# Zero matmuls from the start, two masks by ACT and Pool, and w_in's first columns slot by slot in a retention and gated-MLP kernel

## The chip, the cores and the metric

The kernel runs on one core of a Trainium2 chip. The metric is device time in microseconds (us) for the whole launch: 214.74 us is the median of 13 runs before the change, which lie between 213.97 and 215.69 us. The engines are named as the profile names them: PE is TensorE's matmul row and PEld its weight loads, DVE is VectorE, ACT is ScalarE, POOL is GpSimd, and SP is SyncE, which here only issues DMAs.

## The reference, cut to what matters

```python
def _attn_ref(q, k, v):                    # q, k, v: (4, 8, 768, 64)
    gamma = 1.0 - 2.0 ** (-5.0 - np.arange(H))
    scale = 1.0 / np.sqrt(D)
    for t in range(S):
        state = gamma * state + k[:, :, t] (outer) v[:, :, t]
        y[:, :, t] = scale * (q[:, :, t] @ state)

x = y.transpose(0, 2, 1, 3).reshape(3072, 512)
h = x @ w_in                               # (512, 2048)
g = h * np.cos(h)
out = g @ w_out                            # (2048, 512)
```

## The kernel before

The 768 steps of the recurrence are cut into 6 chunks of 128. A **slot** p is one chunk of two of the four batches (b = 0, 1), with all 8 heads: there are 12 slots, and slots 0 and 1 are the first chunks of the two pairs of batches. Two slots make a **group** g of 512 tokens, which is what one matmul of the MLP takes as its moving side. There are 6 groups.

In a slot, q and k are transposed on PE (`t_mm`) and copied out of PSUM by DVE or ACT (`t_copy`, the tile qkt), `a_mm` multiplies k and q to the scores of even and odd heads (j = 0, 1), these are masked, `y_mm` multiplies masked scores and v (and, after the first chunk, adds the state's share), `s_mm` updates the state, and ACT copies y into the tile xt (`y_copy`). In slots 0 and 1 the mask is the table of decays `dec`, v is only cast (`raw_v`, "rv"), and the scaled v (`conv_v`) is made later on Pool for the state. All matmul inputs are bf16.

The MLP of a group takes 16 blocks of 128 columns of w_in. For a block, `f_mm` is four matmuls of 512 tokens (line 401); `h_mm` takes two blocks for one slot's 256 tokens with eight matmuls of 256 (line 422). ACT then makes the cosine (`f_cos`), DVE the product (`f_mul`, `h_mul`, into the tile gt), and `o_mm` multiplies with w_out (line 446).

The work of slots 0 to 5 and of groups 0 and 1 is put in order by `Plan`, a list scheduler that runs while the program is built. Each operation has engines, a cost, predecessors, tokens (7 PSUM banks, 3 cosine buffers, 8 DMA semaphores, one port shared by DVE and POOL) and a rank; the lowest rank that is ready is taken. A unit of `h` or `f` has rank 1000 and more and yields to work of rank below 20 that comes ready within 0.6. What comes out is a fixed order for each engine; on the chip only semaphores hold an instruction back. `COLD` is the time up to which the planner doubles PE's costs. The fourth argument of `run` is the **fill**: between the two times PE gets matmuls on a tile of zeros (`idle_mm`, line 472) wherever nothing is ready, each counted as 0.12. They too stand in the fixed order, and write to a bank that is then overwritten.

The planner knows of loads by assumed landing times: the first four in the list `map(at, ...)` on line 522, the others in the order of `LOADS` from the second argument of `Plan` on. POOL issues the loads of slots 0 to 7 and of the weights: K of slot 0, then Q1, K1, v0, v1 (slots 0 and 1), the first quarter of w_in in two halves (w0a, w0b), the second and third quarters (w1, w2), then q2 and so on. `HOLD` keeps q2 behind the products named by `SPLIT`.

`SPLIT` names masks (p, b, j) that DVE doesn't do: ACT copies the bank to SBUF (`a_save`, line 345) and POOL multiplies with `dec` (`a_late`, line 349). Before the change this is (1, 0, 1) alone. `HALF0` is the number of blocks of w_in that slots 0 and 1 take by `h_mm`, each as soon as its own y is copied; the blocks from `HALF0` to 15 go by `f_mm`, which needs both slots' y. Before the change `HALF0` is 0. From group 2 on, the loop at the end of the function interleaves `f_mm`, `o_mm` and the slots by hand.

Of the kernel before, what the change touches and what calls it, by code (L numbers as in the profile page):

```python
# [28 lines left out]
class Plan:  # L29
# [16 lines left out]
    def add(self, engines, cost, fn, after=(), rank=0.0, take=(), give=(), mode=None,  # L46
            spare=0, mb=0.0, rate=0.0, lag=0.0, name=""):
        op = dict(engines=engines, cost=cost, fn=fn, after=[a for a in after if a], rank=rank,
                  take=take, give=give, mode=mode, spare=spare, mb=mb, rate=rate, lag=lag,
                  n=len(self.ops), start=None, done=None, free=None, name=name)  # L50
        self.ops.append(op)
        return op
# [91 lines left out]
            op["fn"](op["eng"])  # L144


HALF0, SPARE, RF, RM, COLD = 0, 1, 40.0, 40.0, 8.5


@with_exitstack  # L150
def kernel(
# [9 lines left out]
    nc = tc.nc  # L161
    B, H, S, D = q.shape
# [24 lines left out]
    def sb(shape, dt, name):  # L187
        return const.tile(shape, dt, name=name)
# [29 lines left out]
    zero = sb([128, 256], BF16, "zero")  # L218
# [13 lines left out]
    def kb(p):  # L232
        return kx if p == 1 else ks[p % NB]
# [6 lines left out]
    def load(eng, p, names):  # L240

        bp, c = divmod(ORDER[p], NC)
        for n in names.split():
            t, src = SRC[n[0].lower()]
            if len(n) == 1:
                t = (qs[p % NB] if n == "Q" else kb(p)) if n in "QK" else t[p % PRE]
                eng.dma_start(  # L247
                    out=t.rearrange("p b h d -> p (b h) d"),
                    in_=src[ds(2 * bp, 2), :, ds(c * C, C), :].rearrange(
                        "b h t d -> t (b h) d"))  # L250
            else:
                b = int(n[1])
                eng.dma_start(
                    out=t[p % PRE][:, b],
                    in_=src[2 * bp + b, :, ds(c * C, C)].rearrange("h t d -> t h d"))
# [22 lines left out]
    def conv_q(p, b, e):  # L278
        if p < 2:
            copy(e, qs[p % NB][:, b], qf[p % PRE][:, b])  # L280
            return
        ENG[e].tensor_tensor(out=qs[p % NB][:, b], in0=qf[p % PRE][:, b],  # L282
                             in1=bc(gq, ORDER[p] % NC), op=ALU.mult)

    def conv_v(p, b, e):
        ENG[e].tensor_tensor(out=vb(p)[:, b], in0=vf[p % PRE][:, b],  # L286
                             in1=bc(gk, ORDER[p] % NC), op=ALU.mult)

    def raw_v(p, b, e):
        copy(e, vr[p][:, b], vf[p % PRE][:, b])  # L290

    def conv_k(p, b, e):
        copy(e, ks[p % NB][:, b], kf[p % PRE][:, b])
# [41 lines left out]
    def a_mask(p, b, j):  # L335
        bank = held["a", p, b][j]
        nc.vector.tensor_tensor(  # L337
            out=am[p % 2][b][j], in0=bank.rearrange("p (a t) -> p a t", a=HP),
            in1=(dec[:, j] if p < 2 else mask.unsqueeze(1).to_broadcast([128, HP, 128])),
            op=ALU.mult)  # L340
        banks.give(bank)

    def a_save(p, b, j):
        bank = held["a", p, b][j]
        nc.scalar.copy(out=amf[b], in_=bank)
        banks.give(bank)

    def a_late(p, b, j):
        nc.gpsimd.tensor_tensor(out=am[p % 2][b][j],
                                in0=amf[b].rearrange("p (a t) -> p a t", a=HP),  # L350
                                in1=dec[:, j], op=ALU.mult)
# [26 lines left out]
    def has_s(p):  # L378
        return p != 1 and (p == LATE or ORDER[p] % NC < NC - 1)
# [87 lines left out]
            (nc.sync, nc.scalar)[hf].dma_start(  # L467
                out=out[ds(o_row(g, j), C), ts(hf, 256)], in_=o[:, ts(hf, 256)])

    def idle_mm(e):  # L470
        bank = banks.take()
        nc.tensor.matmul(bank[:, :256], lhsT=zero[:, :128], rhs=zero, start=True, stop=True)  # L472
        banks.give(bank)


# [5 lines left out]
                   allow_small_or_imprecise_dtypes=True)  # L481
    load(nc.sync, 0, "q0 q1")
    load(nc.gpsimd, 0, "K")
    nc.vector.memset(lnsc, math.log(scale))
    nc.vector.memset(halfpi, math.pi / 2.0)

    nc.vector.tensor_tensor(
        out=dist.rearrange("p (a b) -> p a b", a=8),
# [10 lines left out]
    for j in range(2):  # L499
        for a in range(HP):  # L500
# [2 lines left out]
    nc.scalar.activation(out=gq, in_=lgp, func=AF.Exp, bias=lnsc)  # L503
    nc.scalar.activation(out=gk, in_=lgp, func=AF.Exp, scale=-1.0)
    nc.scalar.activation(out=lnsc, in_=halfpi, func=AF.Sin)
    nc.vector.memset(zero, 0.0)


    PL = 6
    ASEP = 4  # L510
    CD = "P"
    SPLIT = {(1, 0, 1)}
    HOLD = "q2", "o2"
    plan = Plan({"bank": 7, "cos": 3, "sem": 8, "out": 4, "port": 1}, 6.0)
    add = plan.add
    SB2 = {"D": (0.33, 0.42), "A": (0.49, 0.585)}
    TT = {"D": (0.6, 0.69), "P": (1.03, 1.05)}
    PS = {"D": (0.6, 0.69), "A": (0.49, 0.585)}
    ld = {}
    prev = None  # L520
    at = lambda tm: dict(start=0.0, free=0.0, done=tm, lat=0.0)
    ld["q", 0, 0], ld["q", 0, 1], ld["k", 0, 0], ld["k", 0, 1] = map(at, (3.9, 5.0, 6.5, 6.5))
    LOADS = ["Q1", "K1", "v0", "v1", "w0a", "w0b", "w1", "w2", "q2", "k2", "w3a", "v2", "w3b", "q3", "k3", "v3",
             "o0", "o1", "o2", "o3", "q4", "k4", "v4", "q5", "k5", "v5", "q6", "k6", "v6",
             "q7", "k7", "v7"]
    LAG = {"w1": 0.8}
    pend = []
    for i, x in enumerate(LOADS):
        if x[0] in "qkvQK":
            p = int(x[1:])  # L530
# [6 lines left out]
        elif x[0] == "w":  # L537
# [4 lines left out]
                    mb=(524288e-6 if w else 1048576e-6), rate=(390e-3 if w else 415e-3),  # L542
                    lag=LAG.get(x, 0.0), name=x)
            for f in range(lo // 128, lo // 128 + (2 if w else 4)):
# [7 lines left out]
    T = {}  # L552
# [3 lines left out]
    for p in range(PL + 2):  # L556
        c = ORDER[p] % NC

        for b in range(2):
            if p == 1:  # L560
                T["cq", p, b], T["ck", p, b] = ld["q", p, b], ld["k", p, b]
            else:
                T["cq", p, b] = add("D" if p < 2 else "DP" if p < 3 else "P", SB2 if p < 2 else TT,
                                    lambda e, p=p, b=b: conv_q(p, b, e),
                                    [ld["q", p, b], G("tq", p - NB, b), G("dt", p - NB, 0)],
                                    10 * p + b, [("port", 1)], [("port", 1)], name="cq%d%d" % (p, b))
            if p == 0:
                T["ck", p, b] = ld["k", p, b]
            elif p > 1:
                T["ck", p, b] = add("A", SB2, lambda e, p=p, b=b: conv_k(p, b, e),  # L570
                                    [ld["k", p, b], G("tk", p - NB, b), G("dt", p - NB, 1), G("s", p - NB)],
                                    10 * p + b, name="ck%d%d" % (p, b))
            cd = add(CD if p == 2 else "P", TT, lambda e, p=p, b=b: conv_v(p, b, e),
                     [ld["v", p, b], G("y", p - NB, b), G("s", p - NB)],
                     10 * p + 1.5 + b + (20 if p == 0 else 60 if p == 1 else 0),
                     [("port", 1)], [("port", 1)], name="cv%d%d" % (p, b))
            T["cd", p, b] = T["cv", p, b] = cd
            if p < 2:
                T["cv", p, b] = add("AD"[b], SB2, lambda e, p=p, b=b: raw_v(p, b, e), [ld["v", p, b]],
                                    10 * p + 2.5 + b, [("port", 1)] if b else [], [("port", 1)] if b else [],  # L580
                                    name="rv%d%d" % (p, b))
# [31 lines left out]
        for b in range(2):  # L613
            for j in range(2):
                if (p, b, j) in SPLIT:
                    o = add("A", (0.49, 0.585), lambda e, p=p, b=b, j=j: a_save(p, b, j),
                            [T["a", p, b]], 0, (), [("bank", 1)],
                            name="ms%d%d%d" % (p, b, j))
                    T["m", p, b, j] = add("P", (1.03, 1.05), lambda e, p=p, b=b, j=j: a_late(p, b, j),
                                          [o], 0, [("port", 1)], [("port", 1)],  # L620
                                          name="ml%d%d%d" % (p, b, j))
                    continue
                T["m", p, b, j] = add("D", (0.6, 0.69), lambda e, p=p, b=b, j=j: a_mask(p, b, j),
                                      [T["a", p, b], G("y", p - 2, b)], 10 * p + 1 + b,
                                      (), [("bank", 1)], name="m%d%d%d" % (p, b, j))
# [13 lines left out]
        else:  # L639
            T["y", p, 0] = T["y", p, 1] = add(  # L640
                "E", 2 * yt + 0.25 * (has_s(p)),
                lambda e, p=p: (y_mm(p, 0), y_mm(p, 1), s_mm(p) if has_s(p) else None),
# [41 lines left out]
    for b in range(2):  # L684
        T["cd", 0, b]["after"] += [T["cv", 1, 1]]
        T["cd", 1, b]["after"] += [T["cd", 0, 1]]
    hold["after"] += [T[("m",) + x] for x in SPLIT]
    for j in range(4):
        for part in range(4):
# [6 lines left out]
                                  "full", name="o%d.%d" % (j, part))  # L696
        add("A", (0.49, 0.585), lambda e, j=j: o_out(0, j, e), [T["o", j, 3]], 300, (),
            [("bank", 1)], name="oc%d" % j)
    plan.run({"S": 2.5, "P": 3.2, "A": 5.5, "D": 3.6, "E": 1.0}, COLD, 0.6, (5.0, 16.0, 0.12, idle_mm))
    plan.emit()  # L700

    for p in (PL + 2, PL + 3):
# [30 lines left out]
    for g in range(2, NG + 1):  # L733
        for s in range(16):
            hf, r = divmod(s, 8)
            p = 2 * (g + 1) + hf
# [46 lines left out]
```

## Time and profile before

| what | value |
|---|---|
| median of 13 runs | 214.74 us |
| the profiled execution's own time | 214.35 us |
| its span, first to last instruction | 212.6 us |
| PE busy from 16 to 32 us of the span | 16.00 of 16.00 us |
| DVE busy from 12 to 16 us | 3.55 us |
| POOL busy from 12 to 16 us, then from 16 to 36 us | 1.76 us, then 19.92 us |
| first `f_mm`, by the chain of waits | 18.09 us |
| fifth `f_mm` (block 4), by the same chain and the spacing in it | 21.9 us |

The time outside the span, 214.35 - 212.6 = 1.75 us, belongs to the launch and isn't covered by the trace. A busy PE says little here before 18 us, because the matmuls on zeros count as busy. The useful work is found by line: 308 (transposes), 331 (scores), 362 and 367 (y), 387 (state), 401 and 422 (w_in), 446 and 463 (w_out); line 472 is the zeros.

### The profile page before, as it was taken

The numbers are of one execution on the slowest core, as the hardware profiler recorded it, in microseconds if no ns is written. First come the engines' busy times: TensorE is split into PE (matmuls) and PEld (weight loads), VectorE is DVE, ScalarE is ACT, GpSimd is POOL, SyncE is SP. The second block draws the span as 40 slices with busy tenths as digits, with TensorE's granted clock in tenths as the row PEclk, the third lists the DMA queues.
The fourth block names the chain that finished last, engine by engine and source line by source line (L and its number), as shares of the span: only waits on it lengthen the run. The fifth ranks groups of instructions, "written<-read, shape, count | busy, mean of one in ns | idle before, by whom it ended". The sixth has DMA issues, their size and how long they took to land.

```text
span 212.6 us, 4219 instructions
## 1 busy us (share of the span) xinstructions
PE 202.7 (95%) x1694; PEld 111.5 (52%) x1694; DVE 115.8 (54%) x199; ACT 115.9 (55%) x193; POOL 78.7 (37%) x83
## 2 busy tenths in 40 slices
PE   1799999999999999999999999999999999999993
PEld 1585456798565445445445445445445444444462
DVE  6492899977845635735736736637633333333000
ACT  7475787788663247437447547545545444554120
POOL 8939999999997006533333000000000000000000
PEclk9999999999999999999999999999999999999999
DMA  7999999999997289999993412311011101110212
GB/s 121 199 249 236 299 325 209 222 345 341 345 189 214 85 194 246 240 215 278 149 255 113 96 49 68 85 49 54 0 49 49 52 0 49 49 51 3 99 65 83
DMA packets 57492, 32.00 MB, mean 151 GB/s; under 512 B 46592, under 2 KB 51968, under 8 KB 57472
## 3 DMA queue, kind: packets, MB, share of 16 engines
q0 software_dynamic: 14352, 15.47, 33.0%
q1 hardware_dynamic: 42976, 16.13, 30.8%
q8 instruction: 13, 0.21, 0.4%
q10 hardware_dynamic: 144, 0.13, 0.2%
q14 instruction: 7, 0.06, 0.1%
HBM read 27.26 MB, written 6.29 MB: 158 GB/s over the span
## 4 chain that ended last, share of the span: by engine, by line
PE 92%; ACT 2%; DMA 2%; DVE 1%; issue 1%; SPq 0%; DVEq 0%
PE bank L446 38%; PE bank L401 32%; PE bank L422 5%; PE bank L331 3%; PE bank L472 3%; PE bank L308 3%; PE bank L362 3%; PE bank L367 3%; DMA qf<-in_q_dram 2%; PE bank L463 2%; PE st_ps L387 1%; ACT cosb L409 1%; ACT ks L271 1%; DVE qs L273 1%; ACT xt L271 0%
## 5 line engine op out<-in xcount | busy, mean ns | idle before, releaser
L409 ACT ACTIVATE cosb<-bank,halfpi 128x512 bf16<-128x512 f32 x96 | 65.3, 687 | 59.1 <-PE bank L401 55.3
L446 PE MATMUL bank<-w_out_sb,gt 128*128 128x512 bf16 x368 | 90.9, 379 | 0.0
L413 DVE TENSOR_TENSOR gt<-bank,cosb 128x512 bf16<-128x512 f32 x80 | 54.2, 688 | 58.5 <-ACT cosb L409 58.1
L401 PE MATMUL bank<-xt,w_in_sb 128*128 128x512 bf16 x320 | 80.7, 379 | 0.0
L446 PEld LDWEIGHTS <-gt 128*128 128x128 bf16 x368 | 35.6, 98 | 42.4
L401 PEld LDWEIGHTS <-w_in_sb 128*128 128x128 bf16 x320 | 30.5, 98 | 35.2
L286 POOL TENSOR_TENSOR vs<-vf,gk 128x512 bf16<-128x512 f32 x22 | 22.7, 1046 | 10.8 <-DMA vf<-in_v_dram 4.4
L282 POOL TENSOR_TENSOR qs<-qf,gq 128x512 bf16<-128x512 f32 x18 | 18.5, 1044 | 21.7 <-DMA qf<-in_q_dram 21.6
L337 DVE TENSOR_TENSOR am<-bank,mask 128x512 bf16<-128x512 f32 x40 | 24.9, 681 | 1.2 <-PE bank L331 1.0
L271 ACT COPY ob<-bank 128x512 f32<-128x512 f32 (+1 forms) x24 | 13.8, 577 | 17.5 <-PE bank L446 15.9
L273 DVE CAST stb<-st_ps 64x512 bf16<-64x512 f32 x17 | 11.7, 686 | 11.6 <-PE st_ps L387 11.4
L271 ACT CAST xt<-bank 128x512 bf16<-128x512 f32 x24 | 12.9, 589 | 8.7 <-PE bank L367 8.7
L422 PE MATMUL bank<-xt,w_in_sb 128*128 128x256 bf16 x128 | 15.1, 273 | 0.5 <-ACT xt L271 0.5
L422 PEld LDWEIGHTS <-w_in_sb 128*128 128x128 bf16 x128 | 12.2, 98 | 2.0 <-issue 0.6
L271 ACT CAST ks<-kf 128x512 bf16<-128x512 f32 x20 | 11.5, 621 | 0.2 <-DMA kf<-in_k_dram 0.2
L430 DVE TENSOR_TENSOR gt<-bank,cosb 128x512 bf16<-128x512 f32 x16 | 10.4, 683 | 2.2 <-ACT cosb L409 2.2
L308 PE MATMUL bank<-ident,qs 128*128 128x128 bf16 x48 | 5.2, 250 | 5.5 <-DVE qs L273 5.5
L362 PE MATMUL bank<-qkt,stb 128*64 128x128 bf16 x160 | 10.3, 222 | 0.0
L367 PE MATMUL bank<-am,vs 128*64 128x128 bf16 x160 | 10.0, 219 | 0.0
L362 PEld LDWEIGHTS <-stb 128*64 128x64 bf16 x160 | 8.7, 110 | 2.4 <-issue 1.9
L247 POOL DMA_DIRECT2D vf<-in_v_dram x8 | 9.4, 1182 | 0.0
L367 PEld LDWEIGHTS <-vs 128*64 128x64 bf16 x160 | 8.9, 110 | 0.0
(59 smaller groups left out, 116.8 us busy)
## 6 DMA issues: line engine op xcount, KB each, us to landing
out_dram<-ob SPq DMA_DIRECT2D x23, 256.0 KB, 2.0
vf<-in_v_dram POOLq DMA_DIRECT2D x8, 512.0 KB, 8.3
qf<-in_q_dram POOLq DMA_DIRECT2D x6, 512.0 KB, 9.3
kf<-in_k_dram POOLq DMA_DIRECT2D x6, 512.0 KB, 9.2
w_out_sb<-in_moe_w_out_dram POOLq DMA_DIRECT2D x4, 512.0 KB, 10.2
qf<-in_q_dram SPq DMA_DIRECT2D x4, 512.0 KB, 4.7
kf<-in_k_dram SPq DMA_DIRECT2D x4, 512.0 KB, 6.5
vf<-in_v_dram SPq DMA_DIRECT2D x4, 512.0 KB, 6.7
```

Source lines behind the costliest of these rows:

```text
L271: nc.scalar.copy(out=out, in_=in_)
L273: ENG[e].tensor_copy(out=out, in_=in_)
L282: ENG[e].tensor_tensor(out=qs[p % NB][:, b], in0=qf[p % PRE][:, b], in1=bc(gq, ORDER[p] % NC), op=ALU.mult)
L286: ENG[e].tensor_tensor(out=vb(p)[:, b], in0=vf[p % PRE][:, b], in1=bc(gk, ORDER[p] % NC), op=ALU.mult)
L337: nc.vector.tensor_tensor(out=am[p % 2][b][j], in0=bank.rearrange("p (a t) -> p a t", a=HP), in1=(dec[:, j] if p < 2 else mask.unsqueeze(1 ...
L362: nc.tensor.matmul(yp[ts(j, 64), a, :], lhsT=stb[p % 2][:, b, a, ts(j, 64)], rhs=qt(n, b, a), start=True, stop=False, skip_group_check=True)
L367: nc.tensor.matmul(yp[ts(j, 64), a, :], lhsT=v_[:, b, 2 * a + j, :], rhs=am[p % 2][b][j][:, a, :], start=(c == 0), stop=True, skip_group_c ...
L401: nc.tensor.matmul(bank, lhsT=w_in_sb[:, i, ts(f, 128)], rhs=xt[g % 2][:, i, :], start=(i == 0), stop=(i == KIN - 1))
L409: nc.scalar.activation(out=cb, in_=bank, func=AF.Sin, bias=halfpi)
L413: nc.vector.tensor_tensor(out=gt[g % 2][:, f, :], in0=bank, in1=cb, op=ALU.mult)
L422: nc.tensor.matmul(bank[:, ts(e, 256)], lhsT=w_in_sb[:, i, ts(f + e, 128)], rhs=xt[g % 2][:, i, ts(hf, 256)], start=(i == 0 and e == 0), s ...
L446: nc.tensor.matmul(bank, lhsT=gt[g % 2][:, f, ts(j, 128)], rhs=w_out_sb[:, f, :], start=(f == 0), stop=(f == KOUT - 1))
```

## The change

The tile of zeros is set before the other small constants, and seven matmuls on it, each 512 columns wide (the zeros read twice over), are put on PE ahead of the plan. The planner's PE starts at 4.2 instead of 1.0, its doubled cost ends at 5.2 instead of 8.5, and fills are allowed from 4.2 to 18.0 instead of from 5.0 to 16.0. `HALF0` becomes 4: blocks 0 to 3 of w_in are done for slot 0 and slot 1 apart. A second mask, (0, 1, 1), is split between ACT and POOL. The other edits change what the planner assumes: K of slot 0 lands at 7.4 instead of 6.5, the other loads run from 6.5 instead of 6.0, w1 has no additional lag, the POOL product costs 1.1 to 1.2 instead of 1.03 to 1.05; and slot 2's q is converted on DVE only.

```diff
-HALF0, SPARE, RF, RM, COLD = 0, 1, 40.0, 40.0, 8.5
+HALF0, SPARE, RF, RM, COLD = 4, 1, 40.0, 40.0, 5.2
...
-    def idle_mm(e):
+    def idle_mm(e, n=1):
         bank = banks.take()
-        nc.tensor.matmul(bank[:, :256], lhsT=zero[:, :128], rhs=zero, start=True, stop=True)
+        nc.tensor.matmul(bank[:, : 256 * n].rearrange("p (n t) -> p n t", n=n),
+                         lhsT=zero[:, :128], rhs=zero.unsqueeze(1).to_broadcast([128, n, 256]),
+                         start=True, stop=True)
         banks.give(bank)
...
     load(nc.gpsimd, 0, "K")
+    nc.vector.memset(zero, 0.0)
     nc.vector.memset(lnsc, math.log(scale))
...
-    nc.vector.memset(zero, 0.0)
+    for i in range(7):
+        idle_mm("E", 2)
...
-    CD = "P"
-    SPLIT = {(1, 0, 1)}
+    CQ, CD = "D", "P"
+    SPLIT = {(1, 0, 1), (0, 1, 1)}
...
-    plan = Plan({"bank": 7, "cos": 3, "sem": 8, "out": 4, "port": 1}, 6.0)
+    plan = Plan({"bank": 7, "cos": 3, "sem": 8, "out": 4, "port": 1}, 6.5)
...
-    ld["q", 0, 0], ld["q", 0, 1], ld["k", 0, 0], ld["k", 0, 1] = map(at, (3.9, 5.0, 6.5, 6.5))
+    ld["q", 0, 0], ld["q", 0, 1], ld["k", 0, 0], ld["k", 0, 1] = map(at, (3.9, 5.0, 7.4, 7.4))
...
-    LAG = {"w1": 0.8}
+    LAG = {}
...
-                T["cq", p, b] = add("D" if p < 2 else "DP" if p < 3 else "P", SB2 if p < 2 else TT,
+                T["cq", p, b] = add("D" if p < 2 else CQ if p < 3 else "P", SB2 if p < 2 else TT,
...
-                    T["m", p, b, j] = add("P", (1.03, 1.05), lambda e, p=p, b=b, j=j: a_late(p, b, j),
+                    T["m", p, b, j] = add("P", (1.1, 1.2), lambda e, p=p, b=b, j=j: a_late(p, b, j),
...
-    plan.run({"S": 2.5, "P": 3.2, "A": 5.5, "D": 3.6, "E": 1.0}, COLD, 0.6, (5.0, 16.0, 0.12, idle_mm))
+    plan.run({"S": 2.5, "P": 3.2, "A": 5.5, "D": 3.6, "E": 4.2}, COLD, 0.6, (4.2, 18.0, 0.12, idle_mm))
```

## The prediction

> **What bounds the kernel now.** I read the page's totals, then the chain of waits in order of time, then the timelines of the first 20 us, engine by engine. The totals, and PE's busy tenths in 40 slices of 5.3 us:
>
> ```profile
> span 212.6 us, 4219 instructions
> PE 202.7 (95%) x1694; PEld 111.5 (52%) x1694; DVE 115.8 (54%) x199; ACT 115.9 (55%) x193; POOL 78.7 (37%) x83
> ...
> PE   1799999999999999999999999999999999999993
> ```
>
> PE is busy in every slice but the first, second and last, and its timeline shows only 0.45, 0.18 and 0.15 us of idle between 18 us and the end. So the end comes at the moment when useful matmuls start to flow, plus their sum. What can be won lies ahead of that moment. The chain there (start, length, engine, tile, line):
>
> ```profile
> 5.40 1.10 DVE qs L273
> ...
> 6.55 0.61 PE bank L308 x4
> 7.16 0.85 PE bank L472 x4
> 8.02 0.85 PE bank L308 x8
> 8.87 0.64 PE bank L472 x3
> 9.51 0.96 PE bank L331 x12
> 10.47 0.97 PE bank L308 x8
> ...
> 14.73 1.60 PE bank L472 x13
> 16.33 0.57 PE bank L367 x16
> 16.89 1.20 PE bank L472 x10
> 18.09 2.59 PE bank L401 x12
> ```
>
> From 6.55 us on PE never pauses, so a late instruction delays all behind it: a fill, too, is work in a fixed order. 4 + 3 fills stand at 0.213 us each (0.85/4, 0.64/3), eight transposes cost 0.85 or 0.97; later ten fills take 1.20 (0.12 each), and the chain has eight transposes at 12.18 us in 0.45. The switch is seen in one fill's duration (min/median/max ns) in two windows:
>
> ```profile
> L472 PE MATMUL bank<-zero x4: 421/421/421, 7.6 to 9.1; 128*128 128x256 bf16 x4
> ...
> L472 PE MATMUL bank<-zero x6: 272/273/401, 11.2 to 11.9; 128*128 128x256 bf16 x6
> ```
>
> PE thus runs at half speed up to some 11.4 us, 4.9 us after its unbroken work began. The last useful gap is the 1.20 us of fills before the first `f_mm`: they wait for ACT, which copies slot 1's y in 1.07 us.
>
> ```profile
> 14.24 1.28 POOL L349 TENSOR_TENSOR am<-gt 128x512 bf16<-128x512 f32 x1 [3.85 <-ACT gt L345]
> ...
> 14.55 1.07 ACT L271 CAST xt<-bank 128x512 bf16<-128x512 f32 x2 [0.39 <-PE bank L367]
> ...
> 16.71 1.07 ACT L271 CAST xt<-bank 128x512 bf16<-128x512 f32 x2 [0.57 <-PE bank L367]
> ```
>
> Slot 0's y is in xt at 15.6 us, and the zeros run while nothing may use it. The loads allow an earlier start: issue plus time to landing gives 7.2 us for K of slot 0, 8.9 for Q1, 10.5 for K1, 12.05 for v0, 13.6 for v1, 14.85 for w0a, 16.2 for w0b, 19.5 for w1, 21.85 for w2.
>
> **The change, part by part.**
>
> *Zeros first.* The memset costs 0.165 us on DVE and goes into DVE's wait for Pool's iota (idle 0.30 us before 1.20), so nothing moves. Seven matmuls of 512 columns cost twice a half-speed fill, 0.43 us, 3.0 together: from about 1.1 to 4.1 us. The first transposes wait for the cast of q until 4.31 anyway. Cover gone, each tenth of overrun is a tenth on the first transposes, which have 1.2 us to spare before the second q arrives. When does full speed come? By the row, 4.9 us after 1.1: at 6.0 us, provided the hole ahead of 6.55 us (some 0.9 us in which PE has run out of planned fills) does no harm. The Trainium skill, "TensorE: Matmul & The Clock Gate", Part 1, speaks against counting on a time: the gate watches a free-running window of about 3.4 us, so opening comes one to two windows after steady work starts, at 4.5 to 7.9 us, and if the hole spoils a window, one later. This trace can't show the phase; its 4.9 us lies inside one to two windows. With the row, everything from 6.55 us on is at full speed. With 7.9, the fills from 6.77 to 7.9 run half as fast: about 5 instead of 9, so 4 x 0.12 = 0.5 us later; with the spoiled window (some 9.9 us) the 14 fills and the eight transposes pay 14 x 0.09 + 0.4 = 1.7 us, which eats the gain. I take the row.
>
> *PE's order up to block 4, by count from the code and duration from the chain.* The second q's transposes stay at 6.55 us (cast of 1.09 us after a landing at 5.38), 0.22 long at full speed (the row at 26.34). The planner believes them done near 5.7 and K at 7.4: (7.4 - 5.7)/0.12 = 14 fills, 1.7 us. So K's transposes start at 8.45 (8.02 before, because K is now assumed later) and end at 8.9, as before. About 4 fills and the scores of slot 0 (0.55, the row at 13.17) end at 9.95 instead of 10.47; Q1's transposes at 10.4 instead of 11.44; 9 fills to the assumed K1; K1's transposes end at 12.0 instead of 12.63; slot 1's scores end near 13.1 instead of 13.73. Every landing above is earlier than its user here. The real order runs about 1.0 us behind the planner's, for it starts 1.08 late and fills cost on the chip what they are counted at.
>
> *The second split mask.* It takes one of DVE's seven masks (0.62 us spacing) away. ACT's copy costs 0.58 in a stretch where ACT has 1.99 us idle before 11.05. Pool's product costs 1.28 (the row above) in Pool's gap of 3.85 us between its loads and 14.24. If the plan puts it ahead of w1 or w2, these are issued behind it and behind its wait for ACT: at some 11.6 us instead of 8.9. w1 landed 10.6 us after issue because the queue was full; a load into a shorter queue took 6.1 (w3a, half as large). 11.6 + 6.1 + 1.7 for the other half (an estimate from w0b and w1, 3.3 us apart) is 19.4, so still no loss. The skill's "SBUF — State Buffer" page (the architecture section on the shared pair) has Pool's product lock out DVE's fast copies. The row: three DVE masks beside the product took 679 to 692 ns, like the others, so masks don't suffer; but the cast at 5.40 took 1.09 instead of 0.43. Cost between 0 and 0.66 us, by the masks' row 0, since DVE has just lost 0.62 us of work.
>
> *Blocks 0 to 3 by slot.* Four `f_mm` (4 x 0.86 = 3.46) become four `h_mm` of eight matmuls (0.87 to 0.89 by 16 in 1.75 and 48 in 5.36 on line 422): +0.1 us. Four cosines and four products of 512 columns stay four. But slot 0's two units (1.75 us) now lie over ACT's copy of slot 1's y, where ten zeros lay. Slot 1's y needs v1 (13.6), its cast by ACT behind slot 0's copies, and DVE's shorter row of masks: I put it at 16.2 by the planner's order plus 1.0, against 16.33. Then slot 0's units to 18.5, slot 1's to 20.2 and the state's 0.37 ahead of or behind block 4: **block 4 near 20.4 us instead of 21.9**, later than w1's landing (19.5). Gain there: 1.5 us; no less than 0.5 with the late clock, no more than 21.9 - 19.5 = 2.4.
>
> *What is late next.* The same stream of loads feeds slots 2 and 3. Slot 2's y ran at 33.12 us, its v was ready on Pool at 31.6: 1.5 us to spare. Slot 3's last scaled q was ready at 35.2 and used at 37.12, its v at 39.6 and used at 42.27; slot 4's q at 47.8, used at 49.66. So 1.5 us pass through just barely, and w_out units can fill holes after that. I take 0.1 us off for it; bounds 0 and 1.0. The planner's other edits (assumed landings, product cost, q of slot 2, which DVE did already) change only the order and are in these bounds.
>
> Sum: 1.5 - 0.1 - 0.1 = 1.3 us. The profiled execution, 214.35 with span 212.6, would give 213.05 with span 211.3; the median 214.74 gives **213.4 us**.
>
> **The rivals.** *Full speed late* (20%): the hole spoils the window or the phase is bad; 0.5 to 1.7 us go. The median over phases gains about 0.6: 214.1. For it: at full load before, the opening took 4.9 us; against it: 3 us of dense matmuls stand ahead. *More than summed* (12%): PE comes at w1's landing, and the 0.78 us of later idle shrinks: 2.3 us, 212.4. *Hidden anyway* (12%): the stream of loads and Pool's scaled q and v hold slots 2 and 3, PE idles the 1.3 us there: 214.7. For it: Pool is busy 19.92 of the 20 us from 16 to 36; against it: the spare listed. *Slower* (12%): Pool's queue. Two products, each waiting for ACT, stand in it, q2 is held behind both, and everything behind q2 follows. q2 was issued at 15.46. If it goes out more than the 1.5 us of spare later, at 17 us, slot 2's y is later than today; at 18 us it costs 1.0: 215.7. Against it: both copies depend on scores that come 0.5 us earlier. *Forecast* (44%).
>
> **How the numbers follow.** 0.2%, 0.43 us, is about what can be told from no change. Faster: 44 + 12 and four fifths of the 20, 0.72; the rest of that case and the hidden one, 0.16; slower 0.12. The range 212.3 to 215.0 takes in the bounds of the sum and the hidden case, and leaves the slower case and the far end of the gain out. The forecast's own range is 212.8 to 213.9.
>
> **What would show it.** Fills of about 272 ns before 8 us; the scores of slot 0 ended at 10 us; line 422 ahead of line 401, with block 4 near 20.4; q2's issue no later than 15.5; slot 2's y near 31.8. Wrong: fills of 421 ns after 8 us, PE waiting on w_in, or PE idle between 30 and 45 us for ACT's xt or Pool's qs.

## The result and the profile after

The changed kernel takes **212.53 us** (median of 11 runs, 212.24 to 213.00) against 214.34 us for the kernel before, now over 48 runs (212.66 to 215.86). The ratio is 0.9909 with a 95% interval of 0.9889 to 0.9930: 1.95 us faster. The forecast was 1.3 us off 214.74. The direction held, and 212.53 lies within the wide range of 212.3 to 215.0. It lies below the forecast's own range of 212.8 to 213.9, though: the gain was half as large again as summed, and twice the 0.9 us that 213.4 would be against the later median of before. The profiled execution took 212.15 us with a span of 210.4 us (214.35 and 212.6 before). That is 0.4 us below the changed kernel's median, while the profile of before stands at its median, so the two profiles differ by more than the medians do.

The page's totals after:

```profile
span 210.4 us, 4279 instructions
PE 204.8 (97%) x1726; PEld 112.8 (54%) x1726; DVE 116.2 (55%) x199; ACT 115.7 (55%) x193; POOL 80.0 (38%) x84
...
PE   7999999999999999999999999999999999999993
```

PE is busy 2.1 us longer than before in a span that is 2.2 us shorter: busy time with zeros in it is no measure. The chain of waits after (start, length, engine, tile, line), with the stretch in which the forecast placed the gain:

```profile
1.41 6.08 DMA ks<-in_k_dram
...
7.54 0.62 PE bank L308 x8
8.16 0.55 PE bank L472 x5
8.70 0.38 PE bank L331 x8
...
13.63 1.68 PE bank L472 x13
15.31 0.57 PE bank L367 x16
15.88 0.98 PE bank L422 x8
16.86 0.11 PE bank L472
16.97 1.85 PE bank L422 x16
```

The chain no longer starts with slot 0's q but with its K, which lands 6.08 us after its issue; from there on PE's timeline shows no pause before 34.31 us, and the first link is at full speed already. Behind slot 1's y (15.31) stand units of line 422, where the ten zeros of 1.20 us stood. PE's timeline after (start, length, instruction, count, idle before and its cause):

```profile
5.40 0.40 PE L308 MATMUL bank<-ident,qs 128*128 128x128 bf16 x4 [0.27 <-DVE qs L273]
5.63 1.69 PE L472 MATMUL bank<-zero 128*128 128x256 bf16 x14
7.54 0.62 PE L308 MATMUL bank<-ident,ks 128*128 128x128 bf16 x8 [0.21 <-DMA ks<-in_k_dram]
...
19.98 4.27 PE L401 MATMUL bank<-xt,w_in_sb 128*128 128x512 bf16 x19
...
34.31 1.91 PE L422 MATMUL bank<-xt,w_in_sb 128*128 128x256 bf16 x16 [0.21 <-ACT xt L271]
```

The same view of before, with the matmuls that hold block 4 and the first two of the later waits:

```profile
20.99 5.35 PE L401 MATMUL bank<-xt,w_in_sb 128*128 128x512 bf16 x24
...
36.25 1.03 PE L422 MATMUL bank<-xt,w_in_sb 128*128 128x256 bf16 x8 [0.45 <-ACT xt L271]
...
38.02 0.38 PE L308 MATMUL bank<-ident,ks 128*128 128x128 bf16 x4 [0.18 <-DVE qkt L273]
```

The second q's transposes stand at 5.40, not at 6.55; the 14 fills that the forecast counted are there and end before K lands. Block 4 starts at 19.98 in this view (21.85 before, from 20.99 and 0.86), slot 2's y at 31.35 (33.05), and PE's last matmul ends at 206.80 (209.04). So of 2.24 us on PE, 1.87 come ahead of block 4, 0.17 are given back between block 4 and slot 2's y, and **0.54 come behind slot 2's y**, where the waits of 0.45, 0.18 and 0.15 us are down to this one of 0.21.

### The profile page after: what moved, and what is told of

It is laid out like the page before. It is cut to its first block, busy times and chain, and to the rows that moved or that the text cites. A ratio compares the mean times of both kernels' runs of the same rounds, so it can differ in the third digit from the quotient of the medians.

```text
span 210.4 us, 4279 instructions
## 1 busy us (share of the span) xinstructions
PE 204.8 (97%) x1726; PEld 112.8 (54%) x1726; DVE 116.2 (55%) x199; ACT 115.7 (55%) x193; POOL 80.0 (38%) x84
## 4 chain that ended last, share of the span: by engine, by line
PE 85%; DVE 6%; DMA 3%; ACT 3%; issue 2%; POOL 0%; DVEq 0%; POOLq 0%; ACTq 0%
PE bank L446 38%; PE bank L401 27%; PE bank L422 7%; DMA ks<-in_k_dram 3%; PE bank L331 3%; PE bank L367 2%; PE bank L362 2%; DVE gt L413 2%; PE bank L472 2%; ACT cosb L409 2%; PE bank L463 2%; PE bank L308 2%; DVE am L337 2%; PE st_ps L387 1%; DVE qkt L273 1%
## 5 line engine op out<-in xcount | busy, mean ns | idle before, releaser
L401 PE MATMUL bank<-xt,w_in_sb 128*128 128x512 bf16 x304 | 77.1, 379 | 0.0
L401 PEld LDWEIGHTS <-w_in_sb 128*128 128x128 bf16 x304 | 28.8, 98 | 33.7
L273 DVE CAST stb<-st_ps 64x512 bf16<-64x512 f32 x19 | 13.1, 687 | 11.8 <-PE st_ps L387 11.5
L422 PE MATMUL bank<-xt,w_in_sb 128*128 128x256 bf16 x160 | 19.0, 273 | 0.2 <-ACT xt L271 0.2
L422 PEld LDWEIGHTS <-w_in_sb 128*128 128x128 bf16 x160 | 15.2, 98 | 2.4 <-issue 0.3
L472 PE MATMUL bank<-zero 128*128 128x256 bf16 (+1 forms) x62 | 10.9, 314 | 1.2 <-DVE halfpi L488 1.1
```

The lines of the kernel that those rows point to most:

```text
L273: ENG[e].tensor_copy(out=out, in_=in_)
L401: nc.tensor.matmul(bank, lhsT=w_in_sb[:, i, ts(f, 128)], rhs=xt[g % 2][:, i, :], start=(i == 0), stop=(i == KIN - 1))
L422: nc.tensor.matmul(bank[:, ts(e, 256)], lhsT=w_in_sb[:, i, ts(f + e, 128)], rhs=xt[g % 2][:, i, ts(hf, 256)], start=(i == 0 and e == 0), s ...
```

## The experiments

Theory A says that the half-speed stretch is most of the gain, theory B that the blocks by slot and the new order are. Later two more came up, C and D. Each kernel below was timed against the kernel before in the same session. "K" is the start of K's transposes and "block 4" the first `f_mm` of block 4, both in PE's timeline of the profiled execution (in E2, E4, E9, E11 and E12 the record of block 4's first matmul is missing; there it is the start of the state's matmuls ahead of it plus 0.37, the distance in the others); "full speed" is the first moment in the trace's record of the granted clock.

| run | median us (n) | spread us | ratio (95%) | full speed | K | block 4 |
|---|---|---|---|---|---|---|
| before, first profile | 214.34 (48) | 3.2 | | 11.49 | 7.81 | 21.85 |
| E5 before again | 215.33 (1) | | | 11.73 | 7.72 | 21.9 |
| changed | 212.53 (11) | 0.8 | 0.9909 (0.9889-0.9930) | 4.15 | 7.54 | 19.98 |
| E1 zeros alone | 213.49 (22) | 1.5 | 0.9944 (0.9923-0.9965) | 6.93 | 8.17 | 21.5 |
| E2 changed, no seven zeros | 213.52 (22) | 2.8 | 0.9949 (0.9926-0.9972) | 9.71 | 8.79 | 21.5 |
| E3 changed, no blocks by slot | 213.50 (22) | 1.1 | 0.9949 (0.9933-0.9964) | 6.20 | 7.71 | 20.9 |
| E4 changed again | 212.41 (6) | 1.0 | 0.9894 (0.9855-0.9933) | 3.99 | 7.56 | 20.7 |
| E6 blocks by slot alone | 213.58 (22) | 2.8 | 0.9963 (0.9941-0.9984) | 10.39 | 7.42 | 20.39 |
| E7 changed, one split mask | 212.51 (6) | 0.3 | 0.9924 (0.9899-0.9948) | 6.77 | 8.03 | 20.40 |
| E8 changed, old landings | 213.14 (13) | 0.9 | 0.9935 (0.9912-0.9958) | 6.09 | 7.91 | 20.57 |
| E9 changed, second q late | 215.97 (16) | 3.0 | 1.0062 (1.0031-1.0094) | 13.61 | 11.10 | 24.5 |
| E10 landings alone | 213.76 (22) | 2.5 | 0.9975 (0.9953-0.9997) | 10.00 | 8.36 | 22.1 |
| E11 zeros and blocks alone | 212.98 (13) | 2.3 | 0.9948 (0.9923-0.9974) | 4.22 | 7.78 | 20.8 |
| E12 w0b assumed later | 212.98 (16) | 1.0 | 0.9931 (0.9910-0.9952) | 4.30 | 7.50 | 19.9 |
| E13 second q late, hole filled | 214.13 (22) | 0.9 | 0.9988 (0.9968-1.0008) | 4.57 | 9.47 | 21.73 |

**E1, the zeros alone.**

```diff
+    nc.vector.memset(zero, 0.0)          # ahead of lnsc, in the kernel before
...
+    for i in range(7):
+        idle_mm("E", 2)
```

> The kernel before with the zero tile set early and the seven wide zero matmuls ahead of its plan, and nothing else; the order of all other instructions is that of before. Theory A (the half-speed stretch is most of the gain): full speed comes by 5 us instead of 11.5, the first f_mm (18.09 us before) starts near 17.0, and the time is 0.9 to 1.9 us below that of the kernel before (ratio 0.991 to 0.996). Theory B (the blocks by slot and the order are most of it): under 0.5 us, ratio above 0.9975.

Theory A's range holds: 0.97 us by the medians. Full speed came at 6.93 in the profile, not by 5. The first `f_mm` came at 17.56, not at 17.0, since K landed late here (1.41 + 6.7 = 8.1) and only four fills stand ahead of it.

**E2, the changed kernel without the seven zeros.** The loop of seven `idle_mm` is left out.

> The changed kernel without its seven wide zero matmuls; the order of all else stays. Theory A: the 14 fills ahead of slot 0's K run at half speed, 3.0 us instead of 1.7, so K's transposes start near 8.8 us instead of 7.54, and what follows is 1.3 to 2.0 us late: 213.8 to 214.5, ratio 0.997 to 1.001. Theory B: within 0.4 us of the changed kernel, ratio 0.991 to 0.993.

The time, 0.99 us above the changed kernel, lies between the two ranges: short of A's 1.3, far above B's 0.4. The place is the one that A named. PE's timeline of E2:

```profile
4.26 0.61 PE L308 MATMUL bank<-ident,qs 128*128 128x128 bf16 x4 [2.37 <-DVE qs L273]
...
5.80 3.19 PE L472 MATMUL bank<-zero 128*128 128x256 bf16 x14
8.79 1.05 PE L308 MATMUL bank<-ident,ks 128*128 128x128 bf16 x8
```

The same 14 fills take 3.19 us instead of 1.69, and K's transposes start at 8.79 though K had landed by 8.1. Fills are cover only at full speed; at half speed they are a delay of their own.

**E3 and E6, the blocks by slot.** E3 is the changed kernel, and E6 the kernel before, with only this number altered:

```diff
-HALF0, SPARE, RF, RM, COLD = 4, 1, 40.0, 40.0, 5.2
+HALF0, SPARE, RF, RM, COLD = 0, 1, 40.0, 40.0, 5.2
```

> The changed kernel with HALF0 = 0, planned anew, so that blocks 0 to 3 wait for both slots' y. Theory A: the first f_mm waits for ACT's copy of slot 1's y, near 17.0 us, block 4 near 20.8 instead of 20.05: 0.5 to 0.8 us slower than the changed kernel, ratio 0.993 to 0.995. Theory B: 1.2 us or more slower, ratio 0.9965 or above.

> The kernel before with HALF0 = 4 alone, planned anew. Theory A: the start stays at half speed, slot 0's blocks lie over ACT's copy of slot 1's y, gain 0.5 to 1.0 us, ratio 0.995 to 0.998. Theory B: 1.5 us or more, ratio 0.993 or below.

Taking them away costs 1.0 us, adding them alone brings 0.8. Both ratios lie in A's ranges, though E3's loss is somewhat above A's 0.8 us. In E3 ten zeros are back behind slot 1's y (15.89, 1.27 us) and the first `f_mm` stands at 16.99, as expected; block 4 follows 0.9 us later than in the changed kernel.

**E4 and E5, both kernels once more.** No edit.

> The changed kernel once more, as the measure for the others and for the arrival of slot 0's second half of q. If the earlier arrival (4.56 us against 5.36 in the profile of before) belongs to the change, this profile has it by 4.7 again and the ratio is 0.991. If it is chance, it lands anywhere between 4.5 and 5.4.

> The kernel before once more, for its profile. If the late second half of q (landing at 5.36 us) belongs to that kernel, it is late here too; if it is chance, it lands anywhere between 4.5 and 5.4. The start of full speed, 11.49 us in the first profile, may fall elsewhere: theory A has it move by up to 3 us from run to run, and the time with it.

The early arrival isn't the change's. In E5, the kernel before, the second q's transposes stood at 5.40 too, and its landing was 1.26 + 3.5 us. The first profile of before had two things late: the landing, by 0.6 us (1.26 + 4.1), and the cast behind it, which took 1.09 us instead of 0.56 (E5) or 0.68 (changed). In every profile in which nothing delays it they lie between 5.39 and 5.76, except the first profile of before with 6.55. E4 also shows what chance does to the changed kernel: w0b landed late there, PE waited 0.60 us for it, and block 4 stood at 20.7.

**E7, one split mask.** `SPLIT = {(1, 0, 1)}` in the changed kernel.

> The changed kernel with the mask (0, 1, 1) back on DVE, planned anew. If the split carries part of the gain, DVE's four masks of slot 0 end 0.6 us later, slot 1's y with them, and the time rises by 0.4 to 0.6 us (ratio 0.9935 to 0.995). If the loads set slot 1's y (v1 lands near 14.1), no more than 0.2 us (ratio 0.991 to 0.992).

The medians agree (212.51 and 212.41 to 212.53); the ratio lies a little above the expected range, which is within its interval. DVE's timeline of E7 has the reason, though it is v0 rather than v1:

```profile
9.62 2.48 DVE L337 TENSOR_TENSOR am<-bank,gt 128x512 bf16<-128x512 f32 x4 [0.44 <-PE bank L331]
...
12.89 0.43 DVE L273 CAST gt<-vf 128x512 bf16<-128x512 f32 x1 [0.24 <-DMA vf<-in_v_dram]
```

With all four masks of slot 0 on DVE, it is still done in time to wait 0.24 us for v0. The split mask brings nothing that shows; E7's interval leaves room for some 0.5 us either way.

**E8 and E10, the assumed landings.** E8 puts the old ones into the changed kernel, E10 the new ones into the kernel before.

```diff
-map(at, (3.9, 5.0, 7.4, 7.4))   ...   6.5)   ...   LAG = {}
+map(at, (3.9, 5.0, 6.5, 6.5))   ...   6.0)   ...   LAG = {"w1": 0.8}
```

> The changed kernel with the landing times that the planner assumed before (K at 6.5, stream from 6.0, w1 with its lag). Fewer fills then stand ahead of K's transposes (7 instead of 14), and PE waits for K instead. If waits of under a microsecond cost no speed, the time is within 0.3 us of the changed kernel (ratio 0.9895 to 0.9925); if the assumed landings carry part of the gain, 0.5 us or more above it (ratio above 0.993).

> The kernel before with the new assumed landing times alone (K at 7.4, stream from 6.5, w1 without its lag), planned anew. If the assumptions help only together with the zeros, because they put 14 fills ahead of K, which cost 3.0 us at half speed: ratio 0.999 to 1.003. If they help by themselves, as their removal from the changed kernel suggests (0.65 us): ratio 0.996 to 0.998.

The new numbers are worth 0.6 to 0.7 us in the changed kernel, which is the second of the two cases for E8, and 0.65 us by themselves, the second case for E10. In E10's profile the first `f_mm` stands at 18.18, 0.25 us later than in that of before, for the fills ahead of K ran at half speed; slot 2's y stands at 32.60, 0.45 us earlier. What the numbers bring alone is the order behind 18 us: from block 4 to PE's last matmul it is 186.59 us in E10 against 187.19 before, with no wait left in E10 where before had 0.78 us of them. E8 is the counterpart, 187.39 against 186.82 in the changed kernel, with waits of 0.24 and 0.40 instead of 0.21.

**E11, zeros and blocks together** on the kernel before, with the old planner numbers and one split mask; the edits are those of E1 and E6.

> The kernel before with the early zeros and HALF0 = 4, but the old planner numbers and one split mask. If the two effects add (0.97 and 0.78 us alone), 212.6 to 212.8 and ratio 0.991 to 0.9925, so that the rest of the change is worth 0.2 us or less. If they overlap, since both fill the same stretch ahead of w0b's landing, ratio 0.9935 to 0.9955.

By the ratio, 0.9948, the two don't add, but the interval just reaches the range for adding; the median, 212.98, is 1.43 us below that of before, where adding would give 1.75. The reason in its profile isn't the one that was expected (w0b). PE's timeline of E11:

```profile
5.69 0.60 PE L472 MATMUL bank<-zero 128*128 128x256 bf16 x4
7.78 1.03 PE L308 MATMUL bank<-ident,ks 128*128 128x128 bf16 x8 [1.49 <-DMA ks<-in_k_dram]
8.61 0.85 PE L472 MATMUL bank<-zero 128*128 128x256 bf16 x3
9.39 1.04 PE L331 MATMUL bank<-qkt 64*128 64x128 bf16 x16
```

Four fills at full speed (0.60), a wait of 1.49 us for K, and then everything at half speed again. The busy times by window of the same trace (window and its length, then each engine's busy time and count, the granted clock, the DMA share and GB/s) show it:

```profile
4.22:7.64 3.42, 1.46 (x15) 0.87 (x14) 1.45 (x4) 2.94 (x8) 3.42 (x4) 1.00 1.95 129
7.64:11.05 3.41, 3.27 (x34) 2.61 (x35) 1.45 (x3) 0.64 (x2) 2.84 (x4) 0.50 2.01 232
11.05:14.46 3.41, 3.41 (x58) 2.67 (x55) 3.19 (x7) 2.75 (x6) 0.34 (x1) 1.00 1.21 272
```

The clock was granted, taken away and granted again in steps of 3.41 us. So early zeros can lose their effect where the 14 fills that come with K assumed at 7.4 are missing. They don't always: E1, too, has four fills there and a wait of 1.32 us, and kept full speed. That this explains the missing sum in all of E11's runs is not shown, since one profile was taken.

Alone, the zeros, the blocks and the landing times bring 0.97, 0.78 and 0.65 us, 2.4 in all, where the whole change brings 1.95; taken out, they cost 0.99, 0.97 and 0.6. So they overlap by some 0.5 us. The planner's start at 4.2, the end of its doubled cost, the limits of the fills, the product's cost and slot 2's q on DVE only were not tried alone.

**E12, a try at a faster version**: `LAG = {"w0b": 0.8, "w1": -0.8}` in the changed kernel.

> The changed kernel with w0b assumed 0.8 later (and w1 as before), planned anew, a try at a faster version: in one profile of the changed kernel PE waited 0.60 us for w0b in slot 0's second unit. Theory A: PE is fed by the loads at this point, and units that need w0a alone go first: ratio 0.988 to 0.990. Theory B: what the new plan does behind 30 us decides, and it is within 0.5 us of the changed kernel on either side: ratio 0.989 to 0.993.

Just above theory B's range, and no gain: block 4 stands at 19.9, and the new order waits 0.60 us at 27.58 and 0.43 us at 35.89 for copies of qkt. No version beat the changed kernel.

**E9, the second q late, and E13, the hole filled.** In the changed kernel, three memsets on DVE hold back the cast of slot 0's second half of q. E13 adds 14 zero matmuls on PE ahead of that q's transposes.

```diff
+            for i in range(3 * b):                      # E9 and E13, ahead of the cast, slot 0
+                nc.vector.memset(idle, 0.0)
...
+        if (p, b, w) == (0, 1, 0):                      # E13 alone, ahead of the transposes
+            for i in range(14):
+                idle_mm("E")
```

> The changed kernel with three memsets of 1024 columns on DVE ahead of the cast of slot 0's second half of q, so that this cast ends near 6.5 us, as the forecast assumed from the first profile of before, instead of 5.3. Theory A (the mis-sized term of the forecast is this arrival: PE starts its unbroken row from it): second transposes at 6.5, K's transposes at 8.4, block 4 at 20.6 to 21.0 instead of 20.05, time 212.9 to 213.3, ratio 0.993 to 0.995. Theory B (the row is set by the loads of K, K1 and v1, whatever q does): within 0.2 us of the changed kernel, ratio 0.989 to 0.992.

Both theories missed, by far: 3.4 us slower than the changed kernel and slower than the kernel before. PE's timeline of E9 (its lines are 3 higher):

```profile
5.08 0.85 PE L475 MATMUL bank<-zero 128*128 128x256 bf16 x3
7.71 0.61 PE L311 MATMUL bank<-ident,qs 128*128 128x128 bf16 x4 [1.78 <-DVE qs L274]
8.12 3.19 PE L475 MATMUL bank<-zero 128*128 128x256 bf16 x14
11.10 1.06 PE L311 MATMUL bank<-ident,ks 128*128 128x128 bf16 x8
```

The cast ended at 7.66, 1.2 us later than meant, and left a hole of 1.78 us; the 14 fills behind it ran at half speed, and full speed came at 13.61 only. This profile is of the slowest of the 16 runs; five of them lie at 214.11 to 214.66 us and the others at 215.69 to 217.14. Arrival and hole changed together, so E13 keeps the arrival and fills the hole.

> The kernel of the late second q, with 14 more zero matmuls of 256 columns on PE ahead of that q's transposes, so that the hole before it (1.78 us) is covered. Theory C (the hole, not the arrival, cost most: it kept a window of 3.4 us too empty for full speed, and the 14 fills ahead of K then ran at half speed): full speed by 7 us, K's transposes near 9.6 us instead of 11.1, block 4 near 21.5 to 22.2, time 213.6 to 214.4 (ratio 0.996 to 1.000), and the runs lie within 1.2 us. Theory D (the arrival itself, or the memsets on DVE, cost it): within 0.5 us of the kernel without the filling, ratio above 1.003.

Theory C. The same timeline of E13 (lines 6 higher than in the changed kernel):

```profile
7.71 0.40 PE L314 MATMUL bank<-ident,qs 128*128 128x128 bf16 x4 [0.85 <-DVE qs L274]
7.94 1.69 PE L478 MATMUL bank<-zero 128*128 128x256 bf16 x14
9.47 0.61 PE L314 MATMUL bank<-ident,ks 128*128 128x128 bf16 x8
```

The transposes stand at 7.71 in both. With the hole filled, the fills take 1.69 again, K's transposes come 1.63 us earlier, and the median is 1.84 us lower (1.6 by the ratios). All 22 runs of E13 (213.85 to 214.72 us) lie about where E9's five fastest do, so the hole cost nothing in some runs and some 2 us in most. The window's phase would explain that, but only one run of each has a trace. What is left, 214.13 - 212.5 = 1.6 us, is the price of the arrival itself: 2.31 us later q (7.71 against 5.40) gives 1.75 us later block 4.

## Where the prediction was right, and the step that failed

- **What bounds the kernel** was right: with PE without a pause behind it, block 4's start carries through to the end. E7 and E4 have the changed kernel's plan or nearly so, with block 4 later by 0.42 and 0.73 us, and PE's last matmul ends 0.41 and 0.80 us later (207.21 and 207.60 against 206.80).
- **The step that failed is "What is late next".** It put the planner's other edits, "assumed landings" among them, at nothing: they "change only the order and are in these bounds", and the bounds, 0 and 1.0, were of a loss. The landing times alone gained 0.65 us (E10; 0.1 to 1.0 by the interval), and taking them out of the changed kernel cost 0.6 (E8). In the profiles the term has the wrong sign: the forecast took 0.1 us off for later waits and 0.1 for the slower units (which 20.4 for block 4 holds already, so that 0.1 was counted twice), and measured are 0.17 us lost up to slot 2's y and 0.54 us won behind it. So 0.2 us loss was forecast and 0.37 gain measured. The forecast had the 0.78 us of later idle on its list but put it into a rival of 12%, "More than summed", which is the one that came: 0.21 us of it is left. E10 and E8 place this on the order that the new landing times make, while the zeros alone keep the wait of 0.45 us for xt (E1) and the blocks alone have one of 0.57 (E6). What in that order does it stays open, for E3 has the new times and a wait of 0.44. One profile can't settle it either: from block 4 to PE's last matmul, the plan of before took 187.19, 188.06 (E5) and 187.54 us (E1), and that of the changed kernel 186.82, 186.89 (E4) and 187.38 us (E2).
- **The second q's arrival was mis-sized.** The step "The second q's transposes stay at 6.55 us" took one profile's arrival, with its long cast, for the kernel's. It is 5.4 to 5.8 in the others. From it came "K's transposes start at 8.45"; measured 7.54, held by K's landing. E13's slope gives an estimate of what this is worth at block 4: 1.15 x 1.75/2.31 = 0.9 us.
- **From slot 1's y to block 4** the sum was too short: from 16.2 to 20.4 is 4.2 us, measured 15.24 to 19.98, 4.74 us. The state's 0.37 does stand ahead of block 4, which the forecast left open, and one more zero of 0.11. The two errors partly cancel, so block 4 was forecast at 20.4 and came at 19.98. In the terms of the profiles, 1.3 becomes 1.3 + 0.37 (block 4: 1.87 instead of 1.5) + 0.57 (what is late next) = 2.24 us; the runs show 1.95.
- **Full speed at 6.0 us, 4.5 to 7.9 by the rule that the prediction takes from the Trainium skill:** measured 3.99 to 6.93 in the nine profiles with early zeros other than E9's. The rule's picture, a window that runs on its own, was the right one, and the row's "4.9 us after unbroken work" was chance (4.0 in E5: PE unbroken from 7.72, full speed at 11.73). Its lower end is too late by half a microsecond: in E4 full speed came at 3.99, behind a window of which PE was busy for 2.93 us only.
- **"If the hole spoils a window, one later"** was the right danger. It cost 0.27 us of idle in the changed kernel and no window. E9 and E11 are that case made real, one ahead of the second q's transposes, one ahead of K's. The forecast priced it at 1.7 us; the larger hole of E9 cost 1.84 by the medians.
- **The second split mask** was taken at no cost, and the DVE time that it frees won nothing (E7). POOL's product stood between w1 and w2, as feared, at 9.99 us, with 0.34 us of wait; w2 was issued at 11.22 and nothing waited for it.
- **Blocks 0 to 3 by slot** lie over ACT's copy as described. E3 and E6 price them at 1.0 and 0.8 us.
- **The slower rival**, POOL's queue, did not come: q2 was issued at 14.79, ahead of 15.46.

## What to carry to other kernels

Work that only keeps an engine awake stands in the same queue as the rest: count it at the speed it will really run at, and see that it reaches over every wait until the real work is dense, for it loses its use, and turns into a delay, behind the first large hole (here holes of 1.49 and 1.78 us did that, while one of 1.32 did not). Take the arrival of a load from several profiles before a sum starts from it; one profile put it 1.1 us off here. And where a planner makes the order anew, the numbers that it assumes are part of the change: give them a term of their own, and time them alone, for here they brought 0.65 us.

## What the runs showed of the hardware

- The clock's decisions lie 3.41 us apart in E11, as "TensorE: Matmul & The Clock Gate", Part 1, of the Trainium skill says. What it takes can be bracketed by PE's busy share in the window ahead of a decision. The clock opened after windows with 2.93 (E4), 3.09 (changed) and up to 3.41 us of 3.41 busy. It stayed shut after windows with 2.21 (before), 2.45 (E5 and E1) and 2.57 us (E9). Once open, it stayed open over a window with 2.05 us (E1) and shut after one with 1.46 us (E11). So the share that opens it lies between 75 and 86%, and the share that keeps it between 43 and 60%. The windows of these shares are reckoned from the opening in steps of 3.41 us; that the steps hold is seen in the record of the clock, where the long stretch at full speed lasts 201.39, 204.80 or 208.21 us in every trace, which is 59, 60 or 61 steps of 3.4133 us.
- The granted clock in the windows is only known from the first recorded change on. Ahead of it the rows say 1.00, while the fills' 421 ns say half speed.
- DVE's multiply for slot 2's q took 0.68 us twice in the changed kernel's profile, 0.68 and 0.93 us in the first one of before, 1.55 us in E5 and 1.47 us in E13, while POOL was issuing loads in all four. E5's line:

```profile
25.18 1.55 DVE L282 TENSOR_TENSOR qs<-qf,gq 128x512 bf16<-128x512 f32 x1
```

  PE then waited 0.39 us for it (0.46 in E13), and E5 took 215.33 us with nearly the same first `f_mm` as the first profile of before (18.00 and 17.93). What holds it was not tried.
- With early zeros and no large hole the runs of a kernel lie within 0.3 to 1.5 us; without, or with a hole, within 2.3 to 3.2 us. That the window's phase at the start makes the wider spread fits both, but is not shown, since only one run of each kernel has a trace (two of the kernel before and of the changed one).
